# A chain of FFT filter, soft mixture of experts and feed-forward on one core: the block transposition, the softmax sums and the tail reordered

## Chip, cores, metric

One NeuronCore of one Trainium2 chip. The metric is the device time of one execution in microseconds; the kernel before has a median of 2024.19 us over 3 runs (2023.47 to 2024.52).

## The reference, cut to what matters

The input x is 8 sequences (blocks b) of 3072 tokens with 256 features. Three parts follow one another:

```python
X = rfft(x, axis=1); Y = X @ (w_r + i w_i) + (b_r + i b_i)
Y = softshrink(Y, 0.01)                  # real and imaginary part each
x1 = irfft(Y)                            # 24576 tokens in all
logits = x1 @ phi                        # 32 slots
d = exp(logits - max over tokens); d /= d.sum(0) + 1e-9
slot_out = experts(d.T @ x1)             # 8 experts, 4 slots each, relu between w1 and w2
c = exp(logits - max over slots); c /= c.sum(1) + 1e-9
h = (c @ slot_out) @ w_in;  out = (h * tanh(softplus(h))) @ w_out
```

d.sum(0) is over all tokens of all blocks; the kernel keeps a running maximum (`m_run`), a running sum (`d_acc`) and running slot inputs (`s_acc`), rescaled after each block by the factors `ab`.

## The kernel before, in words

**First part (eight blocks, four steps k each, 32 steps).** The discrete Fourier transform of 3072 = 128 x 24 points is two matmul stages: `stage1` over 128, a round trip through DRAM (`sdr`), `stage2` over 24. `stage2` leaves each piece in PSUM; ScalarE rounds it to `xh` (L233) and VectorE subtracts to `xl` (L234), one after the other on the same bank. `linear` multiplies by the weights in six groups (three products, two halves); ScalarE, VectorE (`p`, L265) and GpSimd shrink the result into `yt`. `project` applies phi to the spectrum, `inv1` and `inv2` transform the 32 logits back; between these two, `sturn` transposes a whole block's `st` to `v` on VectorE (L317). `smax1` to `smax3` take the block's maximum (`rm`, `mt`, `mb`) and the exponentials `dx`; `csoft1`, `csoft2`, `ctrans` make the softmax over slots and store it to DRAM (`c_d`). `fwd1`, a round trip through DRAM (`d_load`), `fwd2` and `dturn` transform the exponentials, and `slots` multiplies their spectrum by that of x1 (`ytrans`), so that x1 itself is never made. `dsum` and `dsum2` add the exponentials up over tokens: a VectorE reduction, a copy, and a one-column matmul with `ones`.

**Second part.** `weight_sum`, then `Experts.run` (`up`, `turn`, `down`), whose weights are loaded during the end of the first part. **Third part.** `ffn`: hidden matmuls (L837), the gate on ScalarE, a split in two on VectorE, output matmuls (L867).

**Order.** Nothing is scheduled by itself: every step is given a position with `at(pos, fn, ...)`, in units of k, the list is sorted by position, and each engine executes its instructions in this order. `PA` holds positions relative to a block's or step's start (for block b, 4b + 4 plus the value), `TAIL` those of the last blocks relative to NK = 32. DMAs issued by SyncE stand in one queue (SP), so that one that waits holds those behind it; GpSimd issues the 32 stores of the converted feed-forward weights (`conv`, L558). PSUM is a ring of eight tiles, taken in order of position. SBUF is two stacks of pools, `left` and `right`; the experts' weight tiles `w` (pool `ep`) can be loaded when `right` is closed (`rc`), the expert activations `hs` and the tiles of the last part when `left` is closed.

```python
def sturn(b):                            # L312; position 4b + 4 + tu
    nc.vector.transpose(out=v..., in_=spt[b]...)
def inv2(b):                             # L321; position 4b + 4 + i2
    nc.tensor.matmul(ps, lhsT=f1t, rhs=v[:, 12 * i:12 * i + 12], start=True, stop=True)
```

Of the kernel before, what the change touches and what calls it, by code (L numbers as in the profile page):

```python
# [71 lines left out]
def body(ctx, tc, x, w_r, w_i, b_r, b_i, phi, w1, w2, w_in, w_out, cbig, ct, out, dbg=None, stop=False):  # L72
# [26 lines left out]
    const, yp, cp, sm = lpool("const"), lpool("yp", PA["y"]), lpool("cp"), lpool("sm", 2)  # L99
    bp = ctx_r.enter_context(tc.tile_pool(name="bp", bufs=2, side="right"))  # L100
    xp = ctx_r.enter_context(tc.tile_pool(name="xp", bufs=2, side="right"))
    wp, ytp, lp, cvp = rpool("wp"), rpool("ytp", 2), rpool("lp", 2), rpool("cvp")
    psp = lpool("psp", 8, space=PSUM)

# [3 lines left out]
    tall = const.tile([96, NP * 240], F32, name="tall")  # L108
    t_m = tall[:, 0:NP * 144].rearrange("p (n f) -> p n f", f=144)
    t_t = tall[:, NP * 144:].rearrange("p (n f) -> p n f", f=96)  # L110
    ones = const.tile([128, 1], F32, name="ones")
    ones32 = const.tile([NS, 128], F32, name="ones32")
    s_acc = const.tile([128, D], F32, name="s_acc")
    d_acc = const.tile([128, 1], F32, name="d_acc")
    m_run = [const.tile([128, 1], F32, name=f"m_run{i}") for i in range(2)]
    m_t, ab_t = {}, {}
    wsp = {n: (wp.tile([128, 2, D], F32R, name=n + "h"), wp.tile([128, 2, D], F32R, name=n + "l")) for n in "abc"}
# [13 lines left out]
    def setup():  # L131
        nc.scalar.preload_act_table_set("natural_log_exp_and_others")
        nc.sync.dma_start(out=cb, in_=cbig)
        for j in range(na):
            load_x(0, j)
        load_t(0, 0)
        wst = ytp.tile([128, 6, D], F32, tag="yt", name="wst")
        wrf, wif = wst[:, 0:2], wst[:, 2:4]
        nc.gpsimd.dma_start(out=wrf, in_=w_r.rearrange("(h p) e -> p h e", p=128))
        nc.gpsimd.dma_start(out=wif, in_=w_i.rearrange("(h p) e -> p h e", p=128))  # L140
        nc.gpsimd.dma_start(out=ph, in_=phi.rearrange("(h p) e -> p h e", p=128))
        for i, src in ((0, b_r), (1, b_i)):
            nc.gpsimd.dma_start(out=bias[:, i], in_=src.rearrange("(h p) -> p h", p=128))
        nc.vector.memset(ones, 1.0)
        nc.vector.memset(ones32, 1.0)

        k1_t["w"] = wst
# [90 lines left out]

    def linear(k, eh, m):
        if eh == 0 and m == 0:  # L240
            pool, tag = (bp, "b") if k >= NK - 2 else (ytp, "yt")
            yt_t[k] = pool.tile([128, 2, 8, 2, 48], F32, tag=tag, name="yt")
        xh, xl, yt = xh_t[k], xl_t[k], yt_t[k]
        src, (wh, wl) = ((2, wsp["a"]), (1, wsp["b"]), (0, wsp["c"]))[m]
        w = NC + 2 if m == 0 and k % 4 == 0 else NC
        full = psum([128, NC + 2], "l")
        ps = full[:, 0:w]
        cs = slice(src * NC, src * NC + w)
        es = slice(eh * 128, eh * 128 + 128)
        n = 0  # L250
        for h in range(2):
            for ww, xx in ((wh, xh), (wh, xl), (wl, xh)):
                nc.tensor.matmul(ps, lhsT=ww[:, h, es], rhs=xx[:, h, cs], start=n == 0, stop=n == 5)  # L253
                n += 1
        if m == 0:
            k1_t[eh] = lp.tile([128, NC + 2], F32, tag="k1", name="k1")
            nc.scalar.activation(out=k1_t[eh][:, 0:w], in_=ps, func=AF.Copy)
            if w > NC:
                cs_t[eh] = cs = sm.tile([128, 2, 2], F32, tag="cs", name="cs")
                for i, sc in ((0, 0.5), (1, -0.5)):  # L260
                    nc.scalar.activation(out=cs[:, i], in_=k1_t[eh][:, NC:w], func=AF.Relu, scale=sc, bias=half[:, i, eh:eh + 1])
# [12 lines left out]
        if m == 2 and k % 4 == 0:
            cs = cs_t.pop(eh)
            nc.gpsimd.tensor_sub(yt[:, eh, 0, :, 47], cs[:, 0], cs[:, 1])
# [108 lines left out]
    def csoft1(b):  # L385
        lg = ch[b]
        cm = sm.tile([128, N2], F32, tag="cm", name="cm")
        lf = lg.rearrange("p i j s -> p (i j) s")
        nc.vector.tensor_reduce(cm, lf, axis=AX.X, op=ALU.max)
        nc.vector.tensor_sub(lf, lf, cm[:, :, None].to_broadcast([128, N2, NS]))  # L390
        nc.scalar.activation(out=lg, in_=lg, func=AF.Exp)
        ch[b, 6] = lg

    def csoft2(b):
        ec = ch[b, 6]
# [55 lines left out]
                    ch[b, 0][8 * g + 4 * a + c] = dd[:, c, 32 * g:32 * g + 32]  # L451

    def dsum(b):
        d = ch[b, 1]
        rd = sm.tile([128, NS], F32, tag="rm", bufs=1, name="rd")
        nc.vector.tensor_reduce(rd, d.rearrange("p n s -> p s n"), axis=AX.X, op=ALU.add)
        rd4 = sm.tile([128, 4, NS], F32, tag="rm4", name="rd4")
        nc.vector.tensor_copy(rd4, rd[:, None, :].to_broadcast([128, 4, NS]))
        ch[b, 3] = rd4

    def dsum2(b):
        ps = psum([128, 1], "dsp")
        nc.tensor.matmul(ps, lhsT=ch[b, 3].rearrange("p j s -> p (j s)"), rhs=ones, start=True, stop=True)
        if b == 0:
            nc.vector.tensor_copy(d_acc, ps)
        else:
            ab = ab_t[b]
            nc.vector.tensor_scalar(d_acc, d_acc, ab[:, 0:1], None, op0=ALU.mult)
            nc.vector.scalar_tensor_tensor(d_acc, ps, ab[:, 1:2], d_acc, op0=ALU.mult, op1=ALU.add)

    def evict(b, v, out, ps):
        if v and b == NB - 1:
# [4 lines left out]
    def fwd2(b, g):  # L477
        dd = ch[b, 0]
        ps = psum([128, 2, 96], "dt")
        for i in range(2):  # L480
            for j in range(4):
                q = 8 * g + 2 * j + i
                nc.tensor.matmul(ps[32 * j:32 * j + 32, i], lhsT=dd[q], rhs=t_m[:, q, 0:96],
                                 start=True, stop=True, tile_position=(0, 32 * j))
        dt = cp.tile([128, 2, 96], F32, tag="pt", bufs=2, name="dtt")
        evict(b, g % 2, dt, ps)
        ch[b, 7, g] = dt

# [28 lines left out]
    def weight_sum():  # L517
        nc.vector.tensor_scalar(d_acc, d_acc, 1e-9, None, op0=ALU.add)
        nc.vector.reciprocal(d_acc, d_acc)
        ch["w"] = wsel = sm.tile([128, NS], F32, tag="wsel", bufs=1, name="wsel")  # L520
        nc.vector.tensor_scalar(wsel, sel, d_acc, 1.0 / 1536.0, op0=ALU.mult, op1=ALU.mult)

    def warm(n):
        ps = psum([128, 128], "wm")
# [73 lines left out]
    for b in range(NB):  # L598
        f2 = pos("f2", b)
        for n, f in (("tu", sturn), ("i2", inv2), ("m1", smax1), ("m2", smax2), ("m3", smax3), ("f1", fwd1), ("c1", csoft1),  # L600
                     ("ds", dsum), ("dl", d_load), ("c2", csoft2), ("ds2", dsum2)):
            at(pos(n, b), f, b)
        for g in range(4):
            at(f2 + 0.1 * g if b < NB - 1 else NK + TAIL["f2"][g], fwd2, b, g)
# [92 lines left out]
class Experts:  # L697
# [37 lines left out]
    def run(self, big, psh, pso, sit, ident, sot, load_rest):  # L735
# [3 lines left out]
        hs, ht, so = {}, {}, {}  # L739
        def up(g, q):  # L740
            if q == 0:
                hs[g] = ep.tile([128, FE], F32, tag="hs", bufs=2, name="hs")
            ps = psh.tile([128, 2, 512], F32, tag="h", name="hp")[:, 0]
            for h in range(2):
# [30 lines left out]
        for g in range(2):  # L775
# [3 lines left out]
            for h in range(2):  # L779
# [2 lines left out]
                                      src[:, None, :, :].to_broadcast([128, 4, 4, SPE]))  # L782


PA = dict(y=20, s1=-5.89, s1d=0.3402, lb=-1.91, s2=-1.1, s2d=0.0002, pj=1.18, yt=2.24, ytd=0.0002, tu=1.0, i2=1.17, m1=1.17, m2=1.34, m3=1.51, f1=1.84, c1=1.58, ds=1.76, dl=2.05, c2=2.57, ds2=8.73, f2=2.46, sl=3.2, rc=0.3, cx=3.24, cxd=0.0002, x0=-0.79, x1=0.05, ytl=1.05, x2=1.3, x3=2.7)


TAIL = {
# [10 lines left out]
    "warm": ((0.76, 6),),  # L799
}  # L800


# [132 lines left out]
```

## Time and profile before

| | before |
|---|---|
| median of 3 runs | 2024.19 us |
| profiled execution: time / span | 2020.63 / 2018.9 us |
| PE (TensorE) busy / weight loads | 96% / 80% |
| DVE (VectorE) / ACT (ScalarE) / POOL (GpSimd) busy | 58% / 45% / 10% |
| granted TensorE clock, mean | 0.983 |
| chain that ended last | PE 82%, ACT 7%, DVE 6%, DMA 2%, issue 2% |

The span is from the first to the last instruction. A row of the trace names the engine, the line of the kernel, the operation and its tiles as out<-in. PE is TensorE's matmuls, PEld its weight loads, SPq the queue of DMAs that SyncE issues. A name behind an arrow in brackets says what ended the idle time ahead of the instruction. A granted clock of 1.0 is 2.4 GHz, 0.5 is 1.2 GHz.

### The profile page before, as it was taken

The page shows a single profiled execution, that of the slowest core. Times are in us where ns is not written, and L with a number is a line of the kernel's source. Part 1 is how long each engine was busy: PE and PEld are TensorE (multiplying, and loading weights), DVE is VectorE, ACT ScalarE, POOL GpSimd, SP SyncE. Part 2 cuts the span into 40 slices and gives each one's busy share as a digit, 9 for nine tenths or more (in the row PEclk, how much of TensorE's full clock was granted, in tenths as well). Part 3 has the DMA queues.
Part 4 walks back from the last instruction along what each step waited for, and adds up shares of the span by engine and source line. Part 5 has one row for each costly group of instructions (what it writes and reads, how often), then busy time and mean ns, then how long its engine had stood idle before and what let it go on. Part 6 is the DMA issues. An engine that isn't in the chain of part 4 may idle for free.

```text
span 2018.9 us, 30218 instructions
## 1 busy us (share of the span) xinstructions
PE 1937.6 (96%) x12252; PEld 1611.1 (80%) x12252; DVE 1168.5 (58%) x1753; ACT 912.7 (45%) x1507; POOL 193.0 (10%) x245
## 2 busy tenths in 40 slices
PE   8899998999988889999999999999999999999999
PEld 6677786677766648888888888888888888888887
DVE  3345545455555637666666666666666666666665
ACT  2566676666665424333333333333333333333332
POOL 1222232233232200000000000000000000000000
PEclk9999999999999989999999999999999999999999
DMA  8745555454652383002002001002002002000000
GB/s 246 240 122 160 142 169 155 131 149 136 176 165 68 121 301 80 22 22 53 22 21 53 21 22 42 22 22 53 22 22 53 22 22 53 22 22 22 21 22 22
DMA packets 100139, 164.27 MB, mean 81 GB/s; under 512 B 27280, under 2 KB 66832, under 8 KB 99744
## 3 DMA queue, kind: packets, MB, share of 16 engines
q1 hardware_dynamic: 98064, 157.45, 25.9%
q0 software_dynamic: 1792, 4.76, 0.7%
q8 instruction: 96, 1.57, 0.3%
q14 instruction: 43, 0.35, 0.1%
q10 hardware_dynamic: 144, 0.13, 0.0%
HBM read 98.75 MB, written 63.57 MB: 80 GB/s over the span
## 4 chain that ended last, share of the span: by engine, by line
PE 82%; ACT 7%; DVE 6%; DMA 2%; issue 2%; POOL 1%; ACTq 0%; SPq 0%; DVEq 0%; POOLq 0%
PE o L867 53%; PE h L837 9%; PE l L253 6%; PE s L225 3%; PE s L196 3%; DVE xl L234 3%; ACT xh L233 2%; PE tr L307 2%; ACT cl L271 1%; ACT p L272 1%; PE pp L284 1%; PE sps L506 1%; ACT y L309 1%; PE lps L327 1%; POOL yt L273 1%
## 5 line engine op out<-in xcount | busy, mean ns | idle before, releaser
L867 PE MATMUL o<-whl,gh 128*128 128x512 f32 x3072 | 1082.9, 395 | 0.0
L867 PE MATMUL o<-whl,gl 128*128 128x256 f32 x3072 | 827.9, 280 | 0.0
L843 ACT ACTIVATE g<-h 128x1024 f32<-128x1024 f32 x384 | 394.4, 1027 | 746.5 <-PE h L837 737.7
L867 PEld LDWEIGHTS o<-whl,gh 128*128 128x128 f32 x3072 | 566.5, 188 | 121.5
L867 PEld LDWEIGHTS o<-whl,gl 128*128 128x128 f32 x3072 | 578.5, 188 | 31.5
L852 DVE TENSOR_TENSOR gl<-g,gh 128x1024 fp32r<-128x1024 f32 x384 | 470.1, 1224 | 28.9 <-DVE gh L848 0.9
L848 DVE CAST gh<-g 128x1024 fp32r<-128x1024 f32 x384 | 265.8, 692 | 351.8 <-ACT g L843 351.6
L837 PE MATMUL h<-ctt,mst 128*128 128x512 f32 x768 | 240.8, 395 | 0.0
L234 DVE TENSOR_TENSOR xl<-s,xh 128x432 fp32r<-128x432 f32 (+1 forms) x192 | 106.1, 558 | 155.2 <-ACT xh L233 155.2
L273 POOL TENSOR_TENSOR yt<-cl,p 128x384 f32<-128x384 f32 x124 | 125.2, 1009 | 435.9 <-ACT p L272 283.1
L225 PE MATMUL s<-tall,bt 96*128 96x144 f32 x1024 | 136.5, 293 | 9.7 <-DMA bt<-sdr 5.2
L225 PEld LDWEIGHTS s<-tall,bt 96*128 96x128 f32 x1024 | 134.3, 196 | 13.9 <-issue 12.4
L233 ACT ACTIVATE xh<-s 128x432 fp32r<-128x432 f32 (+1 forms) x192 | 90.8, 490 | 113.0 <-DVE xl L234 77.1
L265 DVE TENSOR_TENSOR p<-l,k 128x384 f32<-128x384 f32 x128 | 70.8, 554 | 118.6 <-PE l L253 66.5
L837 PEld LDWEIGHTS h<-ctt,mst 128*128 128x128 f32 x768 | 121.2, 188 | 17.9 <-DVE mst L824 0.5
L875 DVE TENSOR_TENSOR os<-o,os 128x256 f32<-128x256 f32 x192 | 76.5, 419 | 77.0 <-ACT os L874 77.0
L271 ACT ACTIVATE cl<-p,tup 128x384 f32<-128x384 f32 x124 | 76.3, 615 | 96.7 <-DVE p L265 74.4
L196 PE MATMUL s<-xc,cb 128*128 128x512 f32 x192 | 106.6, 647 | 7.9 <-DMA xc<-in_x_dram 7.6
L874 ACT ACTIVATE os<-o 128x256 f32<-128x256 f32 x192 | 73.6, 384 | 41.4 <-PE o L867 37.6
L272 ACT ACTIVATE p<-p,tlo 128x384 f32<-128x384 f32 x124 | 76.4, 616 | 4.0
L309 ACT ACTIVATE y<-tr 96x512 f32<-96x512 f32 x128 | 66.5, 590 | 21.4 <-PE tr L307 21.4
L307 PE MATMUL tr<-cb,yt 128*96 128x128 f32 x512 | 66.6, 277 | 2.4 <-DVE xl L234 1.5
(187 smaller groups left out, 1521.8 us busy)
## 6 DMA issues: line engine op xcount, KB each, us to landing
bt<-sdr SPq DMA_DIRECT2D x32, 768.0 KB, 8.1
out_dram<-os SPq DMA_DIRECT2D x47, 512.0 KB, 2.6
xc<-in_x_dram SPq DMA_DIRECT2D x42, 512.0 KB, 5.2
sdr<-a SPq DMA_DIRECT2D x42, 512.0 KB, 3.1
ctt<-c_d SPq DMA_DIRECT2D x28, 384.0 KB, 7.3
c_d<-chl SPq DMA_DIRECT2D x16, 384.0 KB, 3.1
w1t<-in_moe_w_dram SPq DMA_DIRECT2D x6, 1024.0 KB, 5.9
w2t<-in_moe_w_dram SPq DMA_DIRECT2D x5, 1024.0 KB, 13.3
```

Source lines behind the costliest of these rows:

```text
L196: nc.tensor.matmul(ps, lhsT=f1, rhs=xs, start=True, stop=True)
L225: nc.tensor.matmul(ps[:, i], lhsT=b_t[k][:, p0 + i, h * 128:(h + 1) * 128], rhs=t_m[:, 8 * g + p0 + i, :], start=True, stop=True)
L233: nc.scalar.activation(out=xh, in_=ps, func=AF.Copy)
L234: nc.vector.tensor_sub(part(xl_t[k]), ps, xh.bitcast(F32))
L253: nc.tensor.matmul(ps, lhsT=ww[:, h, es], rhs=xx[:, h, cs], start=n == 0, stop=n == 5)
L273: nc.gpsimd.tensor_sub(yt[:, eh, :, ri, :], cl, p)
L307: nc.tensor.transpose(ps[:, i, eh], yt[:, eh, 2 * c + i].rearrange("p r f -> p (r f)"), ident)
L837: nc.tensor.matmul(ps[:, i], lhsT=mst[:, f * 128:f * 128 + 128], rhs=ct_t[b][:, 4 * m:4 * m + 4].rearrange("p n t -> p (n t)"), start=True ...
L843: nc.scalar.activation(out=g, in_=h_t.pop(p), func=AF.Mish)
L848: nc.vector.tensor_copy(gh, g)
L852: nc.vector.tensor_sub(gl, g, gh.bitcast(F32))
L867: nc.tensor.matmul(o, lhsT=a[:, i, ts], rhs=w, start=f == 0 and n == 0, stop=f == 15 and n == 1)
```

## The change

`sturn` moves from 1.0 to 0.62 (behind `inv1` of the block's last step, ahead of the next step's later matmul groups). The exponentials' sum is no longer a reduction and a matmul: `dsum` reads it from the constant term of the spectrum that `fwd2` has made (`dtt`), at 2.47 instead of 1.76; `dsum2` and `ones` go, and `weight_sum` gets one small matmul that spreads the 32 sums over partitions. The last four spectra get buffers of their own (`yq`), so that `right` closes, and five experts' weight loads are issued, at 0.19 instead of 0.60. The room comes from a DMA reserve of 2 KB. In the last block the steps are reordered: all of `fwd2` and `dturn` together, the exponential of `csoft1` as a step of its own (`ce`) behind the transposes, `ctrans` behind the last `slots`, no warming matmuls. In the experts `ht` is allocated ahead of `hs`.

```diff
+    yq = ctx_r.enter_context(tc.tile_pool(name="yq", bufs=2, side="right"))
...
-    ones = const.tile([128, 1], F32, name="ones")
...
-    d_acc = const.tile([128, 1], F32, name="d_acc")
+    d_acc = const.tile([NS, 1], F32, name="d_acc")
...
-            pool, tag = (bp, "b") if k >= NK - 2 else (ytp, "yt")
+            pool, tag = (bp, "b") if k >= NK - 2 else (yq, "yq") if k >= NK - 4 else (ytp, "yt")
...
-        nc.scalar.activation(out=lg, in_=lg, func=AF.Exp)
-        ch[b, 6] = lg
+
+    def cexp(b):
+        nc.scalar.activation(out=ch[b], in_=ch[b], func=AF.Exp)
+        ch[b, 6] = ch[b]
...
     def dsum(b):
-        d = ch[b, 1]
-        rd = sm.tile([128, NS], F32, tag="rm", bufs=1, name="rd")
-        nc.vector.tensor_reduce(rd, d.rearrange("p n s -> p s n"), axis=AX.X, op=ALU.add)
-        rd4 = sm.tile([128, 4, NS], F32, tag="rm4", name="rd4")
-        nc.vector.tensor_copy(rd4, rd[:, None, :].to_broadcast([128, 4, NS]))
-        ch[b, 3] = rd4
-
-    def dsum2(b):
-        ps = psum([128, 1], "dsp")
-        nc.tensor.matmul(ps, lhsT=ch[b, 3].rearrange("p j s -> p (j s)"), rhs=ones, start=True, stop=True)
+        d = ch[b, 7, 0][0:NS, 0, 47:48]
         if b == 0:
-            nc.vector.tensor_copy(d_acc, ps)
+            nc.vector.tensor_copy(d_acc, d)
...
-        dt = cp.tile([128, 2, 96], F32, tag="pt", bufs=2, name="dtt")
+        dt = cp.tile([128, 2, 96], F32, tag="pt", bufs=4, name="dtt")
...
-        nc.vector.tensor_scalar(wsel, sel, d_acc, 1.0 / 1536.0, op0=ALU.mult, op1=ALU.mult)
+        wdg = sm.tile([NS, NS], F32, tag="mdg", name="wdg")
+        nc.vector.tensor_scalar(wdg, ident[:NS, :NS], d_acc, SC, op0=ALU.mult, op1=ALU.mult)
+        ps = psum([128, NS], "wb")
+        nc.tensor.matmul(ps, lhsT=ones32, rhs=wdg, start=True, stop=True)
+        nc.vector.tensor_mul(wsel, sel, ps)
...
-PA = dict(... tu=1.0, ... ds=1.76, dl=2.05, c2=2.57, ds2=8.73, ...)
+PA = dict(... tu=0.62, ... ce=1.58, ds=2.47, dl=2.05, c2=2.57, ...)
...
 TAIL = {
-    "yt": {..., -2: (0.63, 0.66, 0.661, 0.68), -1: (0.681, 0.701, 0.721, 0.722)},
-    "sl": {-2: ..., -1: (0.69, 0.71, 0.74, 0.75)},
-    "f2": (0.65, 0.651, 0.671, 0.673), "dt": (0.67, 0.672, 0.70, 0.72),
-    ("cx", -2): 0.30, ("ds2", -3): 0.305, ("ds2", -2): 0.31, ("ds2", -1): 0.76,
+    "yt": {..., -2: (0.63, 0.74, 0.741, 0.76), -1: (0.761, 0.762, 0.78, 0.781)},
+    "sl": {-2: ..., -1: (0.73, 0.75, 0.79, 0.80)},
+    "f2": (0.65, 0.651, 0.652, 0.653), "dt": (0.67, 0.671, 0.672, 0.673),
+    ("cx", -2): 0.30,
...
-    ("ds", -1): 0.635, ("c1", -1): 0.655, ("c2", -1): 0.685, ("cx", -1): 0.73,
-    "ws": 0.77, "ld": 0.70,
-    "rc": 0.60,
+    ("ds", -1): 0.69, ("c1", -1): 0.70, ("ce", -1): 0.775, ("c2", -1): 0.777, ("cx", -1): 0.81,
+    "ws": 0.701, "ld": 0.776,
+    "rc": 0.19,
...
-              (0.601, 1, 6, "w"), (0.602, 1, 7, "w"), (0.603, 2, 0, "w"), (0.604, 2, 1, "w"), (0.605, 2, 2, "w"), (0.69, 2, 3, "b"), (0.723, 2, 4, "b")),
-    "warm": ((0.76, 6),),
+              (0.191, 1, 6, "w"), (0.192, 1, 7, "w"), (0.193, 2, 0, "w"), (0.194, 2, 1, "w"), (0.195, 2, 2, "w"), (0.763, 2, 3, "b"), (0.782, 2, 4, "b")),
+    "warm": (),
...
-    nc = _bacc.Bacc("TRN2", target_bir_lowering=False, num_devices=1)
+    nc = _bacc.Bacc("TRN2", target_bir_lowering=False, num_devices=1, dynamic_dma_scratch_size=2048)
```

## Rows read from the trace of the kernel before

**Rows 1.** Stages: from:to, length, busy time of PE, PEld, DVE, ACT, POOL; PEclk, DMA share, GB/s.
```profile
764.00:2018.90 1254.90, 1250.39 (x6904) 1080.44 (x6903) 794.29 (x962) 463.47 (x577) 0.00 (x0) 1.00 0.09 30
```

**Rows 2.** Waits of PE, longest in total: us, times, longest.
```profile
PE lps L327 <- DVE v L317: 33.9, 8, 6.7
```

**Rows 3.** Timeline around block 4's transposition: start, us, engine, line, [idle before <-releaser].
```profile
469.36 0.51 ACT L299 ACTIVATE st<-iu 128x192 f32<-128x192 f32 x1
471.42 0.43 DVE L551 SCALAR_TENSOR_TENSOR cva<-cvc,cva 128x256 f32<-128x256 f32 x1 [3.35 <-POOL cvc L546]
...
482.12 0.97 DVE L317 STREAM_TRANSPOSE v<-st 128x768 f32<-128x768 f32 x1
483.23 2.90 PE L327 MATMUL lps<-v,cb 128*128 128x384 f32 x4 [4.91 <-DVE v L317]
```

**Rows 4.** Groups on PE, 478 to 487 us (block 4), then 701 to 703 us (last block).
```profile
L327 PE MATMUL lps<-v,cb 128*128 128x384 f32 x4 | 2.9, 880 | 4.9 <-DVE v L317 4.9
...
L327 PE MATMUL lps<-v,cb 128*128 128x384 f32 x4 | 1.6, 512 | 0.3 <-DVE v L317 0.3
```

**Rows 5.** Stages again: behind block 4's wait, and behind the wait in the experts.
```profile
480.00:487.00 7.00, 3.77 (x6) 1.85 (x6) 3.51 (x6) 3.54 (x7) 0.00 (x0) 0.52 0.01 2
736.00:744.00 8.00, 6.87 (x32) 3.00 (x36) 1.34 (x2) 1.68 (x3) 0.00 (x0) 0.57 0.78 264
```

**Rows 6.** Timeline behind block 4's `inv2`.
```profile
484.89 0.49 ACT L328 ACTIVATE lg<-lps 128x384 f32<-128x384 f32 x1
...
487.53 0.29 DVE L345 TENSOR_TENSOR rm<-rm 128x128 f32<-128x128 f32 x1
...
491.34 0.27 PE L350 MATMUL mt<-cb,rm 128*128 128x128 f32 x1
```

**Rows 7.** Groups by shape, whole span: busy us, mean ns, idle before.
```profile
L456 DVE TENSOR_REDUCE rd<-dx 128x32 f32<-128x768 f32 x8 | 12.0, 1497 | 0.0
L463 PE MATMUL dsp<-ones,rd 128*128 128x1 f32 x16 | 2.3, 220 | 0.0
```

**Rows 8.** Timeline around `fwd2` of block 4.
```profile
513.72 0.94 DVE L398 TENSOR_REDUCE cs__5303<-lg 128x24 f32<-128x768 f32 x1
514.64 0.32 ACT L475 ACTIVATE dtt<-dt 128x192 f32<-128x192 f32 x1
```

**Rows 9.** GpSimd's stores (L558): duration min/median/max in ns, first and last start; landing.
```profile
L558 POOL DMA_DIRECT2D win_d<-cvc x16: 583/583/617, 68.7 to 367.9; - x16
...
DMA to landing us min/median/max: 2.0/3.4/7.9
```

**Rows 10.** The SP queue's issues from 700 us on: start, us.
```profile
699.56 0.88 SPq L413 DMA_DIRECT2D c_d<-chl  x2
...
711.62 13.91 SPq L732 DMA_DIRECT2D w2t<-in_moe_w_dram  x5
726.43 3.18 SPq L413 DMA_DIRECT2D c_d<-chl  x2
736.52 2.40 SPq L732 DMA_DIRECT2D raw<-in_moe_w_dram  x3
```

**Rows 11.** Timeline from the last `slots` to the feed-forward's first matmuls.
```profile
727.45 1.58 PE L526 MATMUL wm<-cb 128*128 128x128 f32 x12
...
736.48 1.08 ACT L748 ACTIVATE hs<-hp 128x512 f32<-128x512 f32 x2 [10.29 <-DMA c_d<-chl]
...
737.13 4.32 PE L746 MATMUL hp<-w1t,sit 128*32 128x512 f32 x16 [3.44 <-ACT hs L748]
...
755.02 3.70 PE L819 MATMUL mp<-win,sot 128*128 128x512 f32 x8 [0.32 <-DVE sot L781]
```

**Rows 12.** DMA issues of the page: KB each, median us to landing.
```profile
c_d<-chl SPq DMA_DIRECT2D x16, 384.0 KB, 3.1
```

**Rows 13.** The tile `win` from 690 us on: duration, first and last issue; landing.
```profile
L671 SPq DMA_DIRECT2D win<-win_d x2: 433/2562/4690, 739.0 to 743.7; - x2
...
DMA to landing us min/median/max: 11.3/11.9/12.4
```

More of the change, by code (lines that the diff above doesn't have):

```diff
@@ L143, in setup @@
             nc.gpsimd.dma_start(out=bias[:, i], in_=src.rearrange("(h p) -> p h", p=128))
-        nc.vector.memset(ones, 1.0)
         nc.vector.memset(ones32, 1.0)
@@ L453, in dsum @@
     def dsum(b):
-        d = ch[b, 1]
-        rd = sm.tile([128, NS], F32, tag="rm", bufs=1, name="rd")
-        nc.vector.tensor_reduce(rd, d.rearrange("p n s -> p s n"), axis=AX.X, op=ALU.add)
-        rd4 = sm.tile([128, 4, NS], F32, tag="rm4", name="rd4")
-        nc.vector.tensor_copy(rd4, rd[:, None, :].to_broadcast([128, 4, NS]))
-        ch[b, 3] = rd4
-    def dsum2(b):
-        ps = psum([128, 1], "dsp")
-        nc.tensor.matmul(ps, lhsT=ch[b, 3].rearrange("p j s -> p (j s)"), rhs=ones, start=True, stop=True)
+        d = ch[b, 7, 0][0:NS, 0, 47:48]
         if b == 0:
-            nc.vector.tensor_copy(d_acc, ps)
+            nc.vector.tensor_copy(d_acc, d)
         else:
             ab = ab_t[b]
-            nc.vector.tensor_scalar(d_acc, d_acc, ab[:, 0:1], None, op0=ALU.mult)
-            nc.vector.scalar_tensor_tensor(d_acc, ps, ab[:, 1:2], d_acc, op0=ALU.mult, op1=ALU.add)
+            nc.vector.tensor_scalar(d_acc, d_acc, ab[0:NS, 0:1], None, op0=ALU.mult)
+            nc.vector.scalar_tensor_tensor(d_acc, d, ab[0:NS, 1:2], d_acc, op0=ALU.mult, op1=ALU.add)
     def evict(b, v, out, ps):
@@ L600, in body @@
         for n, f in (("tu", sturn), ("i2", inv2), ("m1", smax1), ("m2", smax2), ("m3", smax3), ("f1", fwd1), ("c1", csoft1),
-                     ("ds", dsum), ("dl", d_load), ("c2", csoft2), ("ds2", dsum2)):
+                     ("ce", cexp), ("ds", dsum), ("dl", d_load), ("c2", csoft2)):
             at(pos(n, b), f, b)
@@ L741, in up @@
             if q == 0:
+                if g == 0:
+                    ht[0] = ep.tile([128, 8, 128], F32, tag="ht", name="ht")
                 hs[g] = ep.tile([128, FE], F32, tag="hs", bufs=2, name="hs")
@@ L750, in turn @@
         def turn(g):
-            ht[g] = big.tile([128, 8, 128], F32, tag="mst", name="ht") if g else ep.tile([128, 8, 128], F32, tag="ht", name="ht")
+            if g:
+                ht[g] = big.tile([128, 8, 128], F32, tag="mst", name="ht")
             for q in range(2):
@@ L782, in run @@
                                       src[:, None, :, :].to_broadcast([128, 4, 4, SPE]))
-PA = dict(y=20, s1=-5.89, s1d=0.3402, lb=-1.91, s2=-1.1, s2d=0.0002, pj=1.18, yt=2.24, ytd=0.0002, tu=1.0, i2=1.17, m1=1.17, m2=1.34, m3=1.51, f1=1.84, c1=1.58, ds=1.76, dl=2.05, c2=2.57, ds2=8.73, f2=2.46, sl=3.2, rc=0.3, cx=3.24, cxd=0.0002, x0=-0.79, x1=0.05, ytl=1.05, x2=1.3, x3=2.7)
+PA = dict(y=20, s1=-5.89, s1d=0.3402, lb=-1.91, s2=-1.1, s2d=0.0002, pj=1.18, yt=2.24, ytd=0.0002, tu=0.62, i2=1.17, m1=1.17, m2=1.34, m3=1.51, f1=1.84, c1=1.58, ce=1.58, ds=2.47, dl=2.05, c2=2.57, f2=2.46, sl=3.2, rc=0.3, cx=3.24, cxd=0.0002, x0=-0.79, x1=0.05, ytl=1.05, x2=1.3, x3=2.7)
 TAIL = {
[4 rows of a table removed]
[4 rows of a table added]
     ("tu", -1): 0.50, ("i2", -1): 0.51, ("m1", -1): 0.52, ("m2", -1): 0.54, ("m3", -1): 0.56, ("f1", -1): 0.58, ("dl", -1): 0.62,
[3 rows of a table removed]
[3 rows of a table added]
     "loads": ((-5.5, 1, 0, "xs"), (-5.0, 1, 1, "xa"), (-1.1, 1, 2, "xh"), (-0.7, 1, 3, "xl"), (-0.1, 1, 4, "xh"), (0.0, 1, 5, "xl"),
[1 row of a table removed]
-    "warm": ((0.76, 6),),
[1 row of a table added]
+    "warm": (),
 }
```

4 rows, old and new, of the table TAIL are left out of this document.

## The prediction

> **What bounds the kernel now.** I read the stages first: from 764 us to the end, in the feed-forward, PE is busy for 1250 of 1255 us at full clock [rows 1], and nothing of the change lies there. What can move is the time before 764 us. There I read PE's waits. One stands out: `inv2`'s matmuls wait for the block transposition, 33.9 us in 8 waits [rows 2]; the last block's is 0.3 [rows 4], so seven waits hold 33.6, or 4.8 each. Then I read the timeline at one of them, block 4 [rows 3]. The transposition needs `st`, written at 469.9. On DVE it stands behind `stage2`'s last subtraction, starts at 482.12 and takes 0.97; PE starts at 483.23 having waited 4.91. So the input is there 12 us before it is used: this is an order, not a shortage. The wait has a second price. Behind it the granted clock of 480 to 487 us is 0.52, which is the 1.2 GHz level for most of the stretch [rows 5], and the four matmuls take 2.9 us against 1.6 in the last block, where the wait was short [rows 4]. PE is busy for 3.77 us of that stretch; at half speed about half of that, 1.8 us, is lost. Last I read the end of the first part: the experts wait for the store of `c_d` [rows 11].
>
> **The change, part by part.**
>
> Transposition at 0.62. In front of it DVE then has only `inv1`'s copy by ACT to wait for. `st` was ready at 469.87, and DVE was idle for 3.35 us until 471.42 [rows 3]; the 0.97 us fit there, so I cost the move at nothing. Without this cover the next subtraction `p` would come up to 0.97 later, 6.8 us over seven blocks. What goes is at most 4.8 + 1.8 = 6.6 us per block, 46 us in seven.
>
> What is late next? PE would start `inv2` at 478.3, but the logits are copied by ACT, which comes to them at 484.89 right behind other work [rows 6], since it is still taking `stage2`'s pieces by turns with DVE. DVE loses the transposition there, so this chain comes 1.0 us sooner: the last maximum (487.53) at 486.5, and `mt`, which transposes it, at about 486.6 instead of 491.34 [rows 6]. PE does its work between (the four matmuls of `inv2` and the projection, turns and one group behind them) by about 485 and then waits some 1.6 us. So 4.7 us of 6.6 are kept at this point; I take 4.4, as ACT still has copies queued up. Bounds: 1.0, when ACT and DVE stay the bound and give only the transposition's own time, and 6.6. I take the value from the chain of block 4, between the two. **Seven times 4.4 is 31 us** (7 to 46).
>
> The exponentials' sum. A DVE reduction of 1.50 us per block goes, and two one-column matmul instructions with 2.3 us of PE in all [rows 7]. PE is the bound around them, so I count **1.5 us**; the reduction on DVE gives cushion, I count nothing. Added is a wait: at 2.47 DVE now needs the first `dtt`, which ACT ends at 514.96, while DVE was free for its next work at 513.72 [rows 8]; it would stand 1.2 us. Queued behind it are `csoft2`, whose result is read much later, and the next `p`, for which ACT waits. The reduction taken out of the same step is longer than this wait, so I set the pair at 0; bounds are 8.7 lost (seven times 1.24) and 10.5 won (seven times 1.5).
>
> The five loads at 0.19 (two of `w1`, three of `w2`) go past the two stores of block 6's `c_d` on the SP queue (699.56), which then stand behind them: the five `w2` issues took 13.9 us [rows 10]. Nobody waits for these stores: their buffers are used again by the last block's `ctrans`, which is now later. POOL's queue has no DMA there any more. The loads themselves fall in a stretch with idle DMA engines.
>
> The tail. Now: `wm` fills 1.58 us ahead of the experts [rows 11]; the `c_d` stores are issued from 726.43 behind five loads that were issued up to 725.5, and land only at 736.5, where the alike ones land in a median of 3.1 us [rows 10, 12]. `hs` and `raw` wait for that [rows 10, 11]: PE stands 3.44 us and then works at a granted clock of 0.57 in 736 to 744 [rows 5], which costs at most 2.9. The weights `win` follow `raw` on the queue; their second half lands at 743.7 + 11.3 = 755.0 at the earliest, just when `mp` starts (755.02) [rows 11, 13]. So both PE and the DMA queue end there. After the change the store comes behind the transposes and slots, some 2 us sooner by the `wm` that is gone and the reduction that held `dtt`, less the transposes of `ctrans` moved in front; and with less in front of it, it lands some 3 to 4 us sooner. `raw`, `win` and `mp` move with it: **5.5 us**. Bounds: 0, if two late loads (0.763, 0.782) again stand in front of the store, and 2 + 3.44 + 2.9 = 8.3.
>
> The smaller DMA reserve: GpSimd's store instructions take 0.58 us each and show no wait for room [rows 9]; there are 32, some 20 us apart, and each lands in 3.4 us. I cost it at 0; the bounds are 0 and 3.4 x 32 = 109 us of GpSimd time (the slower rival). The Trainium skill (Debugging Trainium Hangs, Descriptor Overflow) speaks against a smaller reserve: patterns with too many descriptors for a carve-out of 16 KiB per partition hang; by this rule the sum would be the same wherever the kernel ends, and no row here shows such a case. By the fit of the Trainium skill (DMA: Bandwidth & Descriptors, Anatomy of one DMA), 2.0 us plus bytes over 436 GB/s, one 128 KB store would hold GpSimd for 2.3 us, 74 us for all as an estimate; the trace has 3.4.
>
> Sum: 31 + 1.5 + 0 + 5.5 = 38 us. The profiled execution took 2020.63 us with a span of 2018.9, so 1982.6 and 1980.9; the median of the runs stands 3.6 us above it, so **1986 us**.
>
> **The rivals.**
> *All of it comes back.* The backlog on ACT and DVE is worked off in the cushion, and the clock stays up everywhere: 46 + 1.5 + 8.3 = 56 us, 1968 us. For it: PE has few other waits there. Against: `lg` cannot be copied before ACT has done the pieces in front of it.
> *The wait is replaced.* PE comes early to `mt` and to PSUM tiles that ACT and DVE have not emptied, and only the transposition's own 1.0 us per block is won: 7 + 1.5 + 5.5 = 14 us, 2010 us. For it: `lg` at 484.89 followed ACT's other work with no idle time. Against: DVE stood still ahead of `L551` [rows 3], so its load is not the bound over a whole block.
> *Slower: the small reserve holds GpSimd.* If each of the 32 stores must drain before its instruction ends, GpSimd, which also makes `yt`, stands 2.0 to 3.4 us each time. If it all reached PE, 64 to 109 us against 38 won, 2050 to 2095 us; it turns the sign from 1.2 us per store. Against: the last store is long landed when the next is issued, and GpSimd is 10% busy.
> *The change doesn't do what it says.* The transposition still waits, at its new place, for a late `st`, and holds `p`: then only 1.5 + 5.5 = 7 us, 2017 us. Against: `st` was there 1.55 us before DVE's idle time ended [rows 3].
>
> **How the numbers follow.** Forecast 0.65 (its own range 1976 to 1998: 3.0 to 5.8 us per block), all back 0.12, replaced 0.15, nothing moved 0.03, slower 0.05. About 0.2% is what a measurement of this kernel can tell from no change, 4 us; 2017 is beyond it by little, so part of that case counts as the same. Faster 0.93, same 0.02, slower 0.05. The range holds the forecast's own range, the case of all back and the near part of the replaced wait: 1966 to 2006.
>
> **What would show it.** `lps` should no longer stand among PE's waits but for tenths, and its four matmuls take 1.6 us; a gap of 1 to 2 us should stand ahead of `mt`, none with a fallen clock behind it. If those gaps are 4 us, the wait was replaced. DVE should show about 1.2 us idle ahead of `d_acc` with `dtt` as releaser. L558 should stay at 0.58 us; longer ones mean the reserve. In the tail the idle time of `hs` for `c_d` should be under 4 us. The feed-forward should stay at 1255 us; if it changes, my reading of what bounds it is wrong.

## The result, and the profile after

The changed kernel took 1993.35 us (median of 4 runs, 1992.95 to 1994.88), the kernel before 2023.83 beside it (4 runs, 2020.50 to 2024.52): ratio 0.9854, 95% interval 0.9837 to 0.9871. Forecast were 1986.0, and 1966 to 2006. By the medians 30.5 us are won, by the ratio 29.5, by the spans (2018.9 to 1991.4) 27.5, and the forecast sum was 38.

First the feed-forward, as a stage (columns as in [rows 1]), of the changed kernel:

```profile
736.50:1991.40 1254.90, 1250.44 (x6905) 1080.46 (x6903) 794.34 (x963) 463.15 (x577) 0.00 (x0) 1.00 0.10 30
```

From the first output matmul `o` to the end it is as long as before (1255.0 us in both), and PE as busy in it [rows 1]; all that changed lies ahead of it. PE's waits there, changed kernel (us, times, longest):

```profile
PE mt L349 <- DVE rm L344: 7.5, 8, 2.4
...
PE l L252 <- ACT lg L327: 5.4, 6, 1.1
...
PE wb L516 <- DVE wdg L514: 3.4, 1, 3.4
...
PE lps L326 <- DVE xl L233: 1.5, 3, 0.8
```

The 33.9 us for `v` [rows 2] are gone. In their place stand two short waits per block, for `lg` and for `rm`, and a new one of 3.4 us that comes once, in the tail. Block 4 in the timeline of the changed kernel, to be read against [rows 6]:

```profile
470.78 0.85 ACT L327 ACTIVATE lg<-lps 128x384 f32<-128x384 f32 x2
...
471.30 0.44 PE L252 MATMUL l<-xh,ch 128*128 128x384 f32 x1 [0.87 <-ACT lg L327]
...
472.94 0.29 DVE L344 TENSOR_TENSOR rm<-rm 128x128 f32<-128x128 f32 x1
...
473.38 0.30 PE L349 MATMUL mt<-cb,rm 128*128 128x128 f32 x1 [0.76 <-DVE rm L344]
```

The two waits add up to 1.6 us. Here no fallen clock follows; behind other gaps one does (stages of the changed kernel; the third figure from the end is the granted clock):

```profile
305.00:316.00 11.00, 8.76 (x42) 6.25 (x40) 7.08 (x16) 8.06 (x17) 3.30 (x4) 0.69 0.32 107
...
466.00:476.00 10.00, 8.21 (x63) 5.36 (x63) 6.39 (x18) 7.44 (x18) 1.92 (x3) 1.00 0.34 117
646.00:662.00 16.00, 13.49 (x122) 10.26 (x117) 8.59 (x17) 8.03 (x19) 4.30 (x5) 0.68 0.20 34
690.00:700.00 10.00, 6.62 (x58) 4.28 (x57) 3.39 (x10) 2.43 (x5) 0.00 (x0) 0.83 0.34 118
707.00:715.00 8.00, 7.79 (x65) 2.87 (x69) 1.32 (x3) 1.79 (x3) 0.00 (x0) 1.00 0.73 241
```

In block 2 (first row) and around block 6's `dt`, the matmuls of `fwd2` (third row), part of the stretch is granted 1.2 GHz. The wait in block 6 (timeline, changed kernel):

```profile
650.05 0.86 PE L475 MATMUL dt<-tall,dd 96*32 96x96 f32 x16 [2.51 <-DVE cvc L551]
```

The profile names DVE's `cvc`, which `dt` does not read. It reads `dd`, whose load is issued at 645.5 us and lands 4.4 us later, at 649.9; in e8 the profile names this load ahead of the same matmuls (1.74 us). So this is a wait for the round trip of the exponentials through DRAM. The fourth row is the tail, and the timeline of the changed kernel says what lies ahead of it:

```profile
689.11 1.08 PE L485 MATMUL tn<-cb,dtt 128*96 128x128 f32 x8
...
690.99 0.93 DVE L388 TENSOR_REDUCE cm<-lg 128x24 f32<-128x768 f32 x1
691.96 0.96 DVE L389 TENSOR_TENSOR lg<-lg,cm 128x768 f32<-128x768 f32 x1
...
693.19 0.23 DVE L514 TENSOR_SCALAR wdg<-cb,d_acc 32x32 f32<-32x32 f32 x1
...
693.57 0.37 PE L516 MATMUL wb<-wdg,ones 32*128 32x32 f32 x2 [3.38 <-DVE wdg L514]
693.87 1.54 PE L498 MATMUL sps<-y,dh 96*32 96x256 f32 x16
```

`wb`, `weight_sum`'s small matmul, stands at 0.701 ahead of the last block's `slots`, and it needs `wdg`, which on DVE stands behind `csoft1`. PE waits 3.38 us and works on at a granted clock of 0.56 (694 to 697 us). Further on, the experts' first matmuls `hp` run at full clock (fifth row above, 0.57 before [rows 5]), and the wait of ACT's `hs` for the store of `c_d` is 3.87 us instead of 10.29 [rows 11] (timeline, changed kernel):

```profile
710.17 1.33 ACT L746 ACTIVATE hs<-hp 128x512 f32<-128x512 f32 x2 [3.87 <-DMA c_d<-chl]
...
727.07 1.12 PE L818 MATMUL mp<-win,sot 128*128 128x512 f32 x2 [0.32 <-DVE sot L780]
728.44 1.10 PE L818 MATMUL mp<-win,sot 128*128 128x512 f32 x2 [0.25 <-DMA win<-win_d]
```

To see where time is won I read the start of `linear` in step k, then of `hp`, of `mp` and of the feed-forward's first `o`, in the traces. The table gives them less those of the kernel before, in us; the other rows are runs of the next section.

| | k=5 | 7 | 11 | 15 | 19 | 23 | 27 | 31 | `hp` | `mp` | `o` |
|---|---|---|---|---|---|---|---|---|---|---|---|
| before, at | 135.2 | 183.3 | 267.3 | 352.6 | 438.9 | 524.1 | 607.0 | 686.1 | 730.0 | 755.0 | 763.8 |
| changed | +2.2 | -2.0 | -6.6 | -9.0 | -14.1 | -18.4 | -23.0 | -24.8 | -22.8 | -28.0 | -27.4 |
| e1 | +1.6 | -2.3 | -6.4 | -10.8 | -12.5 | -14.3 | -17.3 | -18.4 | -20.0 | -18.7 | -18.7 |
| e5 | +1.5 | -2.5 | -5.1 | -7.5 | -12.6 | -17.0 | -21.6 | -24.3 | -21.7 | -26.6 | -25.6 |
| e8 | -0.1 | -4.3 | -8.9 | -13.4 | -18.6 | -23.0 | -27.5 | -30.8 | -27.7 | -33.2 | -32.7 |
| e11 | +0.2 | -4.0 | -8.7 | -11.1 | -16.2 | -20.6 | -25.1 | -27.3 | -29.5 | -29.4 | -29.1 |
| e6 | +3.1 | -0.9 | -5.6 | -10.1 | -15.2 | -19.6 | -24.1 | -27.3 | -30.3 | -35.7 | -35.3 |
| e10 | +1.3 | -4.6 | -10.0 | -15.4 | -21.0 | -26.3 | -29.9 | -35.2 | -37.8 | -43.2 | -42.6 |
| e12 | +2.2 | -3.8 | -9.2 | -12.6 | -18.2 | -23.4 | -28.3 | -32.7 | -35.2 | -33.7 | -33.7 |

The first column is how an execution starts, ahead of all that was moved; over all traces it lies between -0.1 and +5.6 us (e3), and I leave it out. Between two columns of steps lies one block's transposition. The changed kernel wins 4.2, 4.6, 2.4, 5.1, 4.3, 4.6 and 1.8 us, 27.0 in all; it loses 2.0 up to `hp` and wins 5.2 from `hp` to `mp`.

### The profile page after: what moved, and what is told of

Read it like the earlier page. It is cut to its first block, busy times and chain, and to the rows that moved or that the text cites. A ratio compares the mean times of both kernels' runs of the same rounds, so it can differ in the third digit from the quotient of the medians.

```text
span 1991.4 us, 30146 instructions
## 1 busy us (share of the span) xinstructions
PE 1930.5 (97%) x12226; PEld 1608.1 (81%) x12226; DVE 1152.4 (58%) x1737; ACT 910.6 (46%) x1507; POOL 192.8 (10%) x245
## 3 DMA queue, kind: packets, MB, share of 16 engines
q1 hardware_dynamic: 98064, 157.45, 26.5%
## 4 chain that ended last, share of the span: by engine, by line
PE 82%; ACT 7%; DVE 5%; DMA 2%; issue 2%; POOL 1%; SPq 0%; ACTq 0%; DVEq 0%; POOLq 0%
PE o L866 54%; PE h L836 9%; PE l L252 6%; PE s L224 4%; PE s L195 3%; DVE xl L233 2%; ACT xh L232 2%; PE tr L306 1%; ACT cl L270 1%; ACT p L271 1%; PE sps L498 1%; ACT y L308 1%; POOL yt L272 1%; DVE p L264 1%; PE pp L283 1%
## 5 line engine op out<-in xcount | busy, mean ns | idle before, releaser
L224 PEld LDWEIGHTS s<-tall,bt 96*128 96x128 f32 x1024 | 134.5, 196 | 13.1 <-issue 12.6
L873 ACT ACTIVATE os<-o 128x256 f32<-128x256 f32 x192 | 73.5, 383 | 41.7 <-PE o L866 37.8
L306 PEld LDWEIGHTS tr<-cb,yt 128*96 128x96 f32 x512 | 54.4, 127 | 19.2 <-DVE xl L233 7.9
```

Of the source, the lines that this page charges most:

```text
L224: nc.tensor.matmul(ps[:, i], lhsT=b_t[k][:, p0 + i, h * 128:(h + 1) * 128], rhs=t_m[:, 8 * g + p0 + i, :], start=True, stop=True)
```

## The experiments

My theory was that the transposition's place gives nearly all, and the tail the rest; the rivals were that the other parts (sum, reserve, early loads) give or take something of their own, and that the new waits for `wdg`, `rm` and `lg` take part back. All edits are to lines of positions, but where said.

**e1: the transposition alone** (kernel before).

```diff
-PA = dict(... tu=1.0, ...)
+PA = dict(... tu=0.62, ...)
```

> The kernel before with the transposition alone moved to 0.62. Theory (the order of the transposition is nearly all of it): the seven waits of lps for v go, PE then loses 1.6 to 2 us per block at the logits' copies and at mt, and the ratio to the kernel before is 0.986 to 0.988 (24 to 28 us). Rival (the reduction of dsum on DVE, left in here, refills the wait): less than half, 0.993 or above.

Measured: 2000.08 us beside 2022.6, ratio 0.9886 (0.9869 to 0.9903): 23 us, just short of the theory's 24 and far from the rival. In the tail nothing has changed in kind (waits of PE, e1):

```profile
PE mt L350 <- DVE rm L345: 7.6, 8, 2.4
...
PE l L253 <- ACT lg L328: 5.1, 6, 1.1
PE hp L746 <- ACT hs L748: 5.0, 1, 5.0
```

The waits for `rm` and `lg` come with the transposition's new place, not with the rest of the change. This trace wins 3.9, 4.1 and 4.4 us in its first three blocks and 1.1 to 3.0 in the others, where its granted clock falls (0.92 in 378 to 400 us, 0.88 in 460 to 480).

**e2: the transposition back** (changed kernel).

```diff
-PA = dict(... tu=0.62, ...)
+PA = dict(... tu=1.0, ...)
```

> The changed kernel with the transposition back at 1.0. Theory: the waits of 4 to 7 us per block stand again, the half clock behind them too, and only the tail and the sums are left: 2 to 5 us, ratio 0.9975 to 0.999. Rival (the other parts carry a large share): 10 us or more, ratio 0.995 or below.

Measured: 2020.22 us, ratio 0.9989 (0.9979 to 0.9998), as the theory had it. Taken out of the changed kernel the part is worth 26.9 us by the medians, put into the old one 23. The wait is back as it was [rows 2], and `wb` still waits (waits of PE, e2):

```profile
PE lps L326 <- DVE v L316: 35.2, 7, 7.2
...
PE wb L516 <- DVE wdg L514: 3.4, 1, 3.4
```

**e3: the 2 KB reserve alone** (kernel before).

```diff
-    nc = _bacc.Bacc("TRN2", target_bir_lowering=False, num_devices=1)
+    nc = _bacc.Bacc("TRN2", target_bir_lowering=False, num_devices=1, dynamic_dma_scratch_size=2048)
```

> The kernel before with the DMA reserve of 2 KB alone. Theory: no difference, ratio 0.999 to 1.001, GpSimd's stores at 0.58 us. Rival (GpSimd waits for room, which would explain 2 us lost early on): stores longer than 0.7 us, 2 us or more slower, ratio above 1.001.

Measured: 2023.68 us, ratio 1.0003 (0.9994 to 1.0013). The reserve costs nothing, and the slower rival falls. In the changed kernel the stores' issues are what they were [rows 9] (duration in ns, min/median/max):

```profile
L554 POOL DMA_DIRECT2D win_d<-cvc x16: 581/582/615, 68.5 to 359.3; - x16
```

**e4: the exponentials' sum alone** (kernel before; `weight_sum` with its `wb` stays at 0.77, no `dsum2`).

```diff
-        d = ch[b, 1]
...
+        d = ch[b, 7, 0][0:NS, 0, 47:48]
...
-PA = dict(... ds=1.76, dl=2.05, c2=2.57, ds2=8.73, ...)
+PA = dict(... ds=2.47, dl=2.05, c2=2.57, ...)
```

> The kernel before with the exponentials' sum taken from the spectrum's constant term at 2.47 (0.69 in the last block), without the one-column matmuls. Theory: DVE's wait for dtt (about 3 us a block) and the reduction saved cancel, PE gains its one-column matmuls: 0 to 3 us faster, ratio 0.9985 to 1. Rival (the new wait holds the next p and costs PE): slower by 2 us or more, ratio 1.001 or above.

Measured: 2019.67 us, ratio 0.9979 (0.9970 to 0.9987), or 4.2 us by the ratio, 2.9 by the medians and 1.7 by the spans. The added wait is there and longer than thought (waits of DVE, e4):

```profile
DVE d_acc L458 <- ACT dtt L464: 16.4, 6, 3.9
```

That is 2.7 us each, and the kernel is not slower for it. Whether what stands behind it on DVE had time to spare, or the reduction that is gone (12.0 us in all [rows 7]) pays for it, this run does not separate.

**e5: the five loads at their old place** (changed kernel; the own buffers stay).

```diff
-    "rc": 0.19,
+    "rc": 0.60,
...
-              (0.191, 1, 6, "w"), (0.192, 1, 7, "w"), (0.193, 2, 0, "w"), (0.194, 2, 1, "w"), (0.195, 2, 2, "w"), ...
+              (0.601, 1, 6, "w"), (0.602, 1, 7, "w"), (0.603, 2, 0, "w"), (0.604, 2, 1, "w"), (0.605, 2, 2, "w"), ...
```

> The changed kernel with the right pools closed, and the five expert loads issued, at 0.60 as before. Theory (the early loads are what shortens the wait of hs for the store of c_d): the wait is back to 8 to 10 us and the time 4 to 6 us above the changed kernel's, ratio to the kernel before 0.987 to 0.989. Rival (the order of the tail alone does it): within 1 us of the changed kernel, 0.985.

Measured: 1992.58 us, ratio 0.9847 (0.9833 to 0.9860), as the changed kernel. Its SP queue:

```profile
676.20 1.82 SPq L721 DMA_DIRECT2D w1t<-in_moe_w_dram  x2
678.08 24.29 SPq L728 DMA_DIRECT2D w2t<-in_moe_w_dram  x5
707.67 0.88 SPq L414 DMA_DIRECT2D c_d<-chl  x2
```

This is the rival's time, but the run moves the loads by little. The first row's two `w1t` and the first three of the second row's five `w2t` are the moved loads; the last two `w2t` are those at 0.763 and 0.782, which stay. Counted from the start of step k=31, the moved ones begin at 14.4 us here and at 12.0 in the changed kernel (673.3 us, where four other `w1t` go ahead of them). The store of `c_d` follows 5.3 us behind the last load and `hs` waits 3.87 us for it, both as in the changed kernel.

**e6: `weight_sum` behind the first `slots`** (changed kernel).

```diff
-    "ws": 0.701, "ld": 0.776,
+    "ws": 0.752, "ld": 0.776,
```

> The changed kernel with weight_sum at 0.752 instead of 0.701, behind the second slots. Theory (PE's 3.4 us ahead of wb are a wait that the matmul's place makes, and the half clock behind it comes from it): the wait is gone, the experts start 3 to 5 us sooner, ratio to the kernel before 0.982 to 0.984. Rival (PE would have waited there for DVE and ACT anyway, or the loads set the end): less than 1 us, 0.985.

Measured: 1986.14 us, ratio 0.9817 (0.9804 to 0.9830), some 7 us faster than the changed kernel. The timeline of e6 shows the same matmul with the slots ahead of it:

```profile
687.26 1.07 PE L498 MATMUL sps<-y,dh 96*32 96x256 f32 x16
688.26 1.08 PE L306 MATMUL tr<-cb,yt 128*96 128x128 f32 x8
689.27 1.07 PE L498 MATMUL sps<-y,dh 96*32 96x256 f32 x16
690.72 0.38 PE L516 MATMUL wb<-wdg,ones 32*128 32x32 f32 x2 [0.38 <-DVE wdg L514]
```

The first `slots` take 1.07 us instead of 1.54. From k=31 to `hp` it wins 3.0 us where the changed kernel loses 2.0, so the wait with the fallen clock behind it cost 5.0 in these traces; another 3.4 us come from the blocks, which the edit does not touch and where this execution's clock stayed up in block 2 (30.4 us won from k=5 to k=31 instead of 27.0). That the clock gives all of what the medians show beyond 5.0 is not shown.

**e7: `inv2` earlier** (changed kernel, `i2=0.86` for 1.17).

> The changed kernel with inv2 at 0.86, ahead of the next stage2, instead of 1.17. Theory (what is left of the block's loss is that the logits' copies stand on ACT behind stage2's pieces): the gaps of PE ahead of the next l group and of mt go, 1.6 us or more in each of seven blocks and the half clock of block 2, so 8 to 14 us faster than the changed kernel, ratio to the kernel before 0.978 to 0.981. Rival (ACT's copies, put in front, delay stage2's pieces as long): within 2 us of the changed kernel, 0.984 to 0.986.

Measured: 1991.77 us, ratio 0.9846 (0.9829 to 0.9862): no gain, which is the rival's time. The wait for `lg` is gone, that for `rm` nearly doubled (waits of PE, e7):

```profile
PE mt L349 <- DVE rm L344: 13.7, 8, 3.1
```

**e8: no own buffers, and the five loads at 0.60** (changed kernel; the last four spectra share `yt`'s buffers again).

```diff
-    yq = ctx_r.enter_context(tc.tile_pool(name="yq", bufs=2, side="right"))
...
-            pool, tag = (bp, "b") if k >= NK - 2 else (yq, "yq") if k >= NK - 4 else (ytp, "yt")
+            pool, tag = (bp, "b") if k >= NK - 2 else (ytp, "yt")
...
-    "rc": 0.19,
+    "rc": 0.60,
```

> The changed kernel with the last four spectra back in the shared buffers and the last five c_d loads back at their old place, 0.60. Theory (the own buffers are what lets those loads go early): the loads of the last weights are issued some 25 us later, the last c_d store lands behind them, hs waits 8 to 10 us for c_d instead of 3.9, and the kernel is 4 to 6 us slower than the changed one, ratio to the kernel before 0.987 to 0.989. Rival (the slots of the tail are bound by something else): within 1 us of the changed kernel, ratio 0.985.

Measured: 1990.81 us, ratio 0.9855 (0.9838 to 0.9871): the rival. The SP queue of e8:

```profile
678.90 0.89 SPq L720 DMA_DIRECT2D w1t<-in_moe_w_dram  x2
679.84 16.51 SPq L727 DMA_DIRECT2D w2t<-in_moe_w_dram  x5
701.66 0.89 SPq L413 DMA_DIRECT2D c_d<-chl  x2
```

The theory's first half holds all the same. The five loads (of the experts' weights, not of `c_d` as I had written) begin at 678.9 us, 23.6 behind the start of k=31, where they begin at 14.4 with the own buffers and the same position (e5) and at 12.0 in the changed kernel: the own buffers let them go some 9 us earlier, the position 0.19 another 2.4. The second half fails: the store of `c_d` still comes 5.3 us behind the last load, and `hs` waits 3.86 us for it. Own buffers and early loads together are worth nothing in this tail, where PE waits for `wdg`; e12 tries them without that wait.

**e9: the maximum's second half later** (the kernel of e6).

```diff
-PA = dict(... m2=1.34, m3=1.51, f1=1.84, ... dl=2.05, ...)
+PA = dict(... m2=1.52, m3=1.68, f1=1.95, ... dl=2.1, ...)
```

> The changed kernel with the weighted sum's step moved back to 0.752, as in e6, and the maximum's second half behind the next group of l (m2 1.52, m3 1.68, f1 1.95, dl 2.1), so that TensorE has work while VectorE finishes rm. Theory (the waits of mt for rm, about 1 us in each block, are on the path): the gap ahead of mt goes and the kernel is 3 to 6 us faster than e6, ratio 0.979 to 0.980. Rival (the chain behind it, dps and dx, or the load of dd, then waits as long): no gain or a loss, ratio 0.981 to 0.983.

In this order `csoft1` and its exponential, at 1.58, work on the logits in place before `smax3` reads them, so `dx` is formed from other values and the results are not the reference's; the instructions are the same in number and shape, and only the times are read here. Measured: 2070.11 us, ratio 1.0235 (1.0214 to 1.0256). The wait for `rm` is gone from PE's list, and this heads it (waits of PE, e9):

```profile
PE dt L475 <- DMA dd<-ddr: 69.8, 7, 12.3
```

The theory's gap did go, but the chain behind it, `dps`, the store and load of `dd` and `dt`, had no slack: 10 us of waiting in each of seven blocks, and the granted clock falls to 0.969 in the mean. That is the rival's mechanism, far beyond the size it gave. I had moved the load's issue with the rest, so how much of the 10 us is `m2`'s alone stays open.

**e10: the maximum's first half and `inv2` ahead of `stage2`** (the kernel of e6).

```diff
-PA = dict(... i2=1.17, m1=1.17, ...)
+PA = dict(... i2=0.86, m1=0.88, ...)
```

> The changed kernel with the weighted sum's step at 0.752, as in e6, and both the second load of the maximum and its first half ahead of stage 2 (i2 0.86, m1 0.88). Theory (mt waits because rm is made too late, which an earlier start mends): the gaps ahead of mt and of l go together, some 2 us in each of seven blocks, the kernel is 8 us or more faster than e6, ratio 0.978 or less. Rival (the maximum's pieces delay stage 2's on ScalarE and VectorE by as much): same as e6, ratio 0.981 to 0.983.

Measured: 1979.40 us (4 runs, 1978.05 to 1982.64), ratio 0.9797 (0.9783 to 0.9812): some 4 us faster than e6 by the ratios, 7.2 by the spans, and the fastest kernel of the study, 14 us under the changed one by the medians and 11.5 by the ratios. Neither theory gave this size: both gaps go, 12.9 us in the changed kernel, but the blocks win only 6.1 us more than e6's, and small waits have come up (waits of PE, e10):

```profile
PE tr L306 <- DVE xl L233: 4.3, 9, 0.6
...
PE l L252 <- ACT a L199: 2.6, 5, 0.8
...
PE lps L326 <- DVE v L316: 2.4, 2, 1.6
```

**e11: transposition and sum, all else as before** (the kernel of e4).

```diff
-PA = dict(... tu=1.0, ...)
+PA = dict(... tu=0.62, ...)
```

> The kernel before with two parts of the change, the transposition at 0.62 and the exponentials' sum from the spectrum; the order of the tail, the buffers, the early loads and the reserve stay as before. What it lacks against the changed kernel is what the tail is worth. Theory (the wait for wdg takes back part of the tail's gain): 2 to 4 us slower than the changed kernel, ratio to the kernel before 0.986 to 0.9875; the two parts alone multiply to 0.9886 x 0.9979 = 0.9865. Rival 1 (the tail is worth the 5.5 us forecast): 0.988 or more. Rival 2 (the wait takes it all back): 0.985 or less.

Measured: 1993.42 us, ratio 0.9858 (0.9845 to 0.9872): what the changed kernel takes, so the medians leave nothing for the tail. The interval holds the theory's lower end as well as the second rival; one trace of each kernel says more. From k=31 to `hp` e11 wins 2.2 us where the changed kernel loses 2.0, and from `hp` to `mp` the changed kernel wins 5.2 and e11 loses 0.1. That leaves 0.8 us for the tail from k=31 to `o`, nearer to the second rival. The timeline of e11 shows what it loses behind `hp`:

```profile
708.07 1.08 ACT L741 ACTIVATE hs<-hp 128x512 f32<-128x512 f32 x2 [12.00 <-DMA c_d<-chl]
```

**e12: e10 without own buffers, early loads and reserve.** The buffers and loads are edited as in e8, and:

```diff
-    nc = _bacc.Bacc("TRN2", target_bir_lowering=False, num_devices=1, dynamic_dma_scratch_size=2048)
+    nc = _bacc.Bacc("TRN2", target_bir_lowering=False, num_devices=1)
```

> The kernel of e10 without the own buffers, the early loads and the 2 KB reserve. Theory (these three parts move nothing): same as e10, ratio 0.9785 to 0.981. Rival (once PE comes sooner to the tail, the experts' loads at their old place are late): PE waits for w1t or w2t, ratio 0.982 or more.

Measured: 1988.71 us, ratio 0.9841 (0.9827 to 0.9854), 9 us slower than e10: parts that were worth nothing in the changed kernel are worth most of that here. The SP queue of e12:

```profile
678.31 13.79 SPq L727 DMA_DIRECT2D w2t<-in_moe_w_dram  x5
694.13 2.06 SPq L413 DMA_DIRECT2D c_d<-chl  x2
```

The SP queue of e10:

```profile
684.21 2.12 SPq L728 DMA_DIRECT2D w2t<-in_moe_w_dram  x2
691.62 0.88 SPq L414 DMA_DIRECT2D c_d<-chl  x2
```

In e10 two loads stand ahead of the store of `c_d`, and it follows them by 5.3 us; in e12 five do, and it follows by 2.0. What waits for it, in the timeline of e12:

```profile
703.06 1.08 ACT L745 ACTIVATE hs<-hp 128x512 f32<-128x512 f32 x2 [9.17 <-DMA c_d<-chl]
```

In e10 this wait is 3.87 us. The landings say why: the last load ahead of it lands at 701.1 us in e12 and the two stores of `c_d` at 702.0 and 703.0, where e10 has 692.9, 694.1 and 695.2. The rival named `w1t` or `w2t` as what PE would wait for; it is the store behind them. From `hp` to `mp` e12 takes 26.5 us (694.8 to 721.3), e10 19.6: 6.9 of the 9 us. The moved loads begin 23.9 us behind the start of k=31 in e12 and 11.7 in e10. Which of the three parts gives this wasn't tried one by one here; e3 speaks against the reserve, and by e5 beside e8 it is the own buffers that let the loads go early, more than their position.

## Why the prediction was right, and where it was off

Direction and range were right, the size was 7 to 10.5 us too good, by medians or spans. In the sum, one bound is off: the upper end of the forecast's own range, 1998, goes with 2.7 us per block and not with 3.0, which changes nothing else. By its own steps:

- **Transposition, 31 us of 4.4 in each of seven blocks** (with the sum 32.5). Right in mechanism: the wait for `v` is gone, `inv2`'s matmuls take 0.49 us in the median, near the last block's mean before (0.51), instead of 0.88 in block 4 [rows 4], and block 4's two waits of 0.87 and 0.76 are the 1.6 us that were forecast, but shared between `l` and `mt`. Where the clock stays up, the size holds too: e8 wins 4.2 to 5.2 in six blocks and 3.3 in the last, 30.7 in all. The sentence that failed is that no gap with a fallen clock behind it would be left. In block 2 the changed kernel wins 2.4 us where e8 wins 4.5, at clocks of 0.69 and 1.00 in 305 to 316 us. In block 6 PE waits 2.5 us ahead of `dt`, for the load of `dd`, with a clock of 0.68 in that stretch. So the blocks won 27.0 instead of 32.5 in this execution, the sum's part included. By the runs the part is worth 23 (e1) to 27 us (e2) instead of 31.
- **Exponentials' sum, 1.5 us, and its wait at no cost.** The wait was mis-sized, 2.7 us in the mean instead of 1.2: in block 4, whose rows I took [rows 8], it is 1.40 in the changed kernel, elsewhere up to 3.9. That the wait and the reduction taken out cost nothing as a pair was right (e4). The gain is 1.7 by the spans, 2.9 by the medians and 4.2 by the ratio, beside 1.5.
- **Early loads at no cost.** Right for the kernel as changed (e5, e8). That they give nothing either holds only while the tail is late; e12, which lacks the buffers behind them too, shows what they hide.
- **Reserve at no cost.** Shown by e3. The Trainium skill (Debugging Trainium Hangs, Descriptor Overflow) warned of patterns with more descriptors than their carve-out holds; no run here shows such a case, and the stores kept their 0.58 us.
- **Tail, 5.5 us.** This is the term that failed. What I named did happen behind `hp`: `hs` waits 3.87 us instead of 10.29, `hp` runs on at full clock (0.57 before [rows 5]), `raw`, `win` and `mp` move up, and 5.2 us are won there. Ahead of `hp` I had `weight_sum`'s position in the diff, 0.77 to 0.701, and its new matmul, and gave the pair neither a row nor a cost. It stands ahead of the slots and needs what DVE makes behind `csoft1`; it took back 5.0 us (e6). A wait that is added was to be asked what is queued behind it, and here that was all that PE does in the tail. Net, the tail is worth 0.1 us by the medians (e11) and 0.8 by the traces, from k=31 to `o`.
- **Rivals.** Neither *all comes back* nor *the wait is replaced* took place as a whole; the second did in small, with 7.5 + 5.4 us of waits for `rm` and `lg` in place of 33.9. *The reserve holds GpSimd* and *nothing moves* are out, by e3 and by e1 and e2.

## What to carry to other kernels

When a diff moves a step, list every instruction it issues with its new neighbours on each engine; the one small matmul that was left out cost what the whole rest of the tail won. When a wait is removed, the next operand in the chain should be moved with it as a group: `inv2` alone earlier gave nothing (e7), with the maximum's first half it gave some 4 us (e10). And a part that measures nothing alone may be hidden behind another wait: try it again once that wait is gone (e8 against e12).

## What the hardware showed that was not expected

The same gaps don't always bring the clock down. The timeline of PE in block 2 of the changed kernel:

```profile
306.34 0.44 PE L252 MATMUL l<-xh,ch 128*128 128x384 f32 x1 [1.09 <-ACT lg L327]
308.42 0.30 PE L349 MATMUL mt<-cb,rm 128*128 128x128 f32 x1 [0.76 <-DVE rm L344]
309.11 0.87 PE L294 MATMUL iu<-tall,phat 96*32 96x96 f32 x16 [0.39 <-ACT y L308]
```

The same stretch of e6:

```profile
307.38 0.44 PE L252 MATMUL l<-xh,ch 128*128 128x384 f32 x1 [1.09 <-ACT lg L327]
309.46 0.30 PE L349 MATMUL mt<-cb,rm 128*128 128x128 f32 x1 [0.77 <-DVE rm L344]
310.15 0.54 PE L294 MATMUL iu<-tall,phat 96*32 96x96 f32 x16 [0.39 <-ACT y L308]
```

These three waits agree to 0.01 us, yet the sixteen `iu` matmuls behind them take 0.87 us in one and 0.54 in the other, and the granted clock of 305 to 316 us is 0.69 and 1.00. Up to the last block the two programs issue the same instructions in the same order, since e6 moves `weight_sum` alone. The clock of this stretch was 1.00 in e1 and e8 as well, 0.69 in e11 and 0.73 in e5. So a block with such gaps is worth some 2 us more or less from one execution to the next (2.4 us won in block 2 of the changed kernel, 4.5 in e6's), and a single trace can't tell that from an effect of the change. The Trainium skill (TensorE: Matmul & The Clock Gate, What's actually happening) says that the window in which the gate looks at activity runs freely and isn't reset when a kernel starts. That would fit two executions with the same gaps and different clocks, though no run here shows the window itself.
